# The steady part of a fused attention and FFN kernel: a written order, states times W_in four chunks at a time, softmax rows turned by 32x32 blocks and DMA

## The chip, the cores and the metric

The kernel runs on one core of a Trainium2 chip. The metric is the device time of one execution in microseconds. A core has a matrix engine (TensorE, PE in the profile, with its weight loads as PEld), a vector engine (VectorE, DVE), a scalar engine (ScalarE, ACT), and SyncE (SP), which here only issues DMA transfers; ScalarE can issue transfers too. Each engine works through its own list of instructions in order and waits on semaphores that other engines and transfers raise. TensorE writes to PSUM, which has eight banks of 128 x 512 fp32; everything else lies in SBUF.

## The reference

There are 8 batches. In each, 8 heads hold 512 tokens and 32 states of 64 numbers. Tokens read the states, states read the tokens, and all rows then go through one FFN with W_in (512 x 2048), a bounded square and W_out (2048 x 512):

```python
scores = scale * x @ state.T             # (512, 32) per head
a = softmax(scores);  xread = a @ state
a2 = softmax(scores.T); sread = a2 @ x   # (32, 512) @ (512, 64)
rows = concatenate([xread, sread])       # 544 rows per batch, 512 wide
h = rows @ w_in
g = where(h >= 1, h, where(h <= -1, 0, (h + 1) ** 2 / 4))
out = g @ w_out
```

The result has 4352 rows of 512 in fp32. The kernel keeps this precision by splitting operands into a high part (fp32r) and the rest, and by adding three products: high x high, high x low, low x high.

## The kernel before

**The work of a batch.** The states are multiplied by W_in first, so that `a @ (state @ w_in)` takes the place of `(a @ state) @ w_in`. W_in has 8 chunks of 256 columns. `sw_product` (L416) makes states x W_in for `n` chunks: 16 small matmuls (64 x 32) per chunk into the PSUM tile `sw`, which has the tag "mm" (one buffer of two banks). `sw_high` (L436, ScalarE) and `sw_low` (L440, VectorE) split it into two SBUF tiles, of which there are two pairs. In the steady part a pair of chunks is made at a time, `sw_make(nb, nj, 2)`.

**The FFN.** A step (b, j) treats 256 of the 2048 hidden columns of batch b, so a batch has 8 steps. `g1` (L509) makes two products of 6 matmuls into two PSUM banks (tag "h", two buffers), then on ScalarE relu of each and one square of both, on VectorE `bound` of each (it reads the h bank a last time), then `high` (ScalarE) and `low` (VectorE). `g2` (L520) multiplies the result of the step before by W_out: 24 matmuls into four PSUM banks (tag "acc", four buffers). After the last step of a batch, `store` (L547) copies each acc bank to SBUF on ScalarE and sends it out through ScalarE's DMA queue.

**The attention of the next batch** runs beside the FFN in pieces, the generator `Attention.steps` (L379): scores into mm (16 matmuls, `sc`); VectorE's 32x32 block transposes, the softmax over states, and the transpose back give the tokens' side (`ath`, `atl`); maximum and exponential straight from the scores give the states' side `e2`. `turn2` (L327) turns `e2` in 8 TensorE transposes (128 x 128) into the mm banks (`e2p`), `keep_turned` copies it back to SBUF on ScalarE, `read2` (L342) multiplies it by the tokens in 64 small matmuls (`sr`), `scale2` (VectorE) divides by the sums, `keep2` (L365) is one TensorE transpose (`rt`), and `keep` copies it into `srT`. For batches 2 to 7 `sr` and `rt` lie in h banks. The states' rows of all 8 batches go through the FFN at the end as "batch 8" (four steps; there W_in itself is split by `wi_split`, L449).

**What sets the order.** The start (batch 0 and the attention of batch 1) is laid out by a planner, `Plan`, and issued in its order inside `tc.manual_schedule()`. The steady part (L794 to L827) is issued after that block has been closed: the loop gives the instructions, and the framework's scheduler places them on each engine. A step is g1, then g2 of the step before, then `between_steps`: an sw pair after every even step, and one piece of attention after steps 1, 3, 4 and 6. SP's queue carries the loads of the next batch (`load_xt`, `load_xn`, issued at step 0).

Of the kernel before, what the change touches and what calls it, by code (L numbers as in the profile page):

```python
# [137 lines left out]
def state_exchange_moe(  # L138
# [27 lines left out]
    NJ = NF // 2  # L166
# [45 lines left out]
    att_of = {}  # L212
# [12 lines left out]
    class Attention:  # L225
# [109 lines left out]
        def keep_turned(self):  # L335
# [3 lines left out]
            nc.vector.tensor_scalar_add(self.r2, self.sum2, 1e-9)  # L339
            nc.vector.reciprocal(out=self.r2, in_=self.r2)  # L340

        def read2(self):  # L342
            b = self.b
            xn = loaded.pop(("xn", b))
            if b < 2:
                sr = self.sr = ps_mm(f"sr{b}")
            else:
                sr = self.sr = ps_h(f"sr{b}").rearrange("p (q f) -> p q f", q=2)
            for q in range(2):
                for t in range(NT):  # L350
                    for pr in range(NPR):
                        c0 = t * P + pr * NS
                        nc.tensor.matmul(  # L353
                            sr[pr * NS:(pr + 1) * NS, q, :D], lhsT=self.e2[:, q, c0:c0 + NS],
                            rhs=xn[:, t, 2 * pr + q], start=t == 0, stop=t == NT - 1,
                        )
# [6 lines left out]
            )  # L363

        def keep2(self):  # L365
            if self.b < 2:
                self.rt = ps_mm(f"rt{self.b}")
            else:
                self.rt = ps_h(f"rt{self.b}").rearrange("p (q f) -> p q f", q=1)
            nc.tensor.transpose(  # L370
                out=self.rt[:, 0, :P], in_=self.rs.rearrange("p a d -> p (a d)"), identity=ident
            )
# [6 lines left out]
        def steps(self):  # L379
            self.scores()  # L380
            for q in range(2):
                self.turn(q)
            for q in range(2):
                self.top2(q)
            for q in range(2):
                self.exp2(q)
            yield
            for f in (self.top1, self.less1, self.exp1, self.sum1, self.inv1, self.norm1):
                for q in range(2):
                    f(q)  # L390
            self.turn2()
            self.keep_turned()
            yield
            for q in range(2):
                self.back(q)
                self.high1(q)
                self.rest(q)
            self.read2()
            self.scale2()
            yield  # L400
            self.keep2()
            self.keep()
            yield

# [6 lines left out]

    sw_of = {}

    def sw_product(b, c, n):  # L416

        pt = ps_mm(f"sw{b}_{c}")
        for i in range(n):
            for pr in range(NPR):  # L420
                for hh in range(2):
                    rows = slice(hh * 64, hh * 64 + 64)
                    nc.tensor.matmul(  # L423
                        pt[pr * NS:(pr + 1) * NS, hh, i * CI:(i + 1) * CI],
                        lhsT=sb[rows, b, pr], rhs=w32[c + i][rows, pr], start=True, stop=True,
                    )
# [4 lines left out]
        sw_of[b, c] = pt[:, :, :w], wh, wl  # L431
        for i in range(n):
            cols = slice(i * CI, (i + 1) * CI)
            chunk[b, c + i] = wh[:, :, cols], wl[:, :, cols]

    def sw_high(b, c):  # L436
        pt, wh, _ = sw_of[b, c]
        nc.scalar.copy(out=wh, in_=pt)

    def sw_low(b, c):  # L440
        pt, wh, wl = sw_of[b, c]
        nc.vector.tensor_tensor(out=wl, in0=pt, in1=wh.bitcast(F32), op=ALU.subtract)

    def sw_make(b, c, n):
        sw_product(b, c, n)
        sw_high(b, c)
        sw_low(b, c)
# [11 lines left out]
    class Hidden:  # L459
# [26 lines left out]
        def relu(self, i):  # L486
            nc.scalar.activation(out=self.u[:, i], in_=self.hs[i], func=AF.Relu, scale=0.5, bias=half)  # L487

        def square(self):
            nc.scalar.activation(out=self.u, in_=self.u, func=AF.Square)  # L490

        def bound(self, i):
            nc.vector.scalar_tensor_tensor(  # L493
# [15 lines left out]
    def g1(b, j):  # L509
        hid = Hidden(b, j)  # L510
        for i in range(2):
            hid.product(i)
            hid.relu(i)
        hid.square()
        for i in range(2):
            hid.bound(i)
        hid.high()
        hid.low()

    def g2(b, j, half=None):  # L520
# [12 lines left out]
        for i, t in pairs:  # L533
            f = 2 * per * j + i
            oh, ol = wo[f // 2][:, 0, f % 2], wo[f // 2][:, 1, f % 2]
            c0 = (i % per) * n + t * P
            lh, ll = (v[:, i // per, c0:c0 + P] for v in (gh, gl))
            a = acc[b][t]
            nc.tensor.matmul(a, lhsT=lh, rhs=oh, start=f == 0, stop=False)  # L539
            nc.tensor.matmul(a, lhsT=lh, rhs=ol, start=False, stop=False)  # L540
            nc.tensor.matmul(a, lhsT=ll, rhs=oh, start=False, stop=f == NF - 1)  # L541
            if last and i == 2 * per - 1:
                store(b, t)
# [3 lines left out]
    def store(b, t):  # L547
        if t == 0:
            outs[b] = rawp.tile([P, NT, DM], F32, tag="raw", name=f"o{b}")
        o = outs[b][:, t]  # L550
        if b == B and t % 2:
            nc.vector.tensor_copy(o, acc[b][t])
        else:
            nc.scalar.copy(out=o, in_=acc[b][t])  # L554
        if b < B:
            r0 = b * TOK + t * P
            nc.scalar.dma_start(out=out[r0:r0 + P, :], in_=o)
        else:
# [85 lines left out]
    atts = {}  # L644
# [140 lines left out]
        if j:  # L785
            g2_ops(0, j - 1, 1)
    sw_ops(1, 0, 2)
    import os
    with guard:
        plan.emit(warm, ("sc", 0, 0), ("g2", 0, 0, 0))  # L790

    steps = [(b, j) for b in range(1, B + 1) for j in range(NJ if b < B else NJ // 2)]  # L794

    def between_steps(b, j):

        if b < B:
            nb, nj = (b, j + 2) if j + 2 < NJ else (b + 1, 0)
            if j % 2 == 0 and nb < B:  # L800
                sw_make(nb, nj, 2)
            if j in (1, 3, 4, 6):
                next(att, None)

    def splits(b, j):
        if b == B:
            for c in (2 * j, 2 * j + 1):
                wi_split(c)

    for i, (b, j) in enumerate(steps):  # L810
        if j == 0:
            if b + 1 < B:
                loaded["xt", b + 1] = load_xt(b + 1)
                loaded["xn", b + 1] = load_xn(b + 1)
                att = Attention(b + 1).steps()
            elif b == B:
                sh, sl = (work.tile([P, NPR, B * NS], F32R, tag=t, name=f"s{t}") for t in ("ath", "atl"))
                src = srT.rearrange("p a b n -> p a (b n)")
                nc.vector.tensor_copy(sh, src)
                nc.vector.tensor_tensor(out=sl, in0=src, in1=sh.bitcast(F32), op=ALU.subtract)  # L820
                att_of[B] = (sh, sl)
        g1(b, j)
        if i + 1 < len(steps):
            splits(*steps[i + 1])
        g2(*(steps[i - 1] if i else (0, NJ - 1)))
        between_steps(b, j)
    g2(*steps[-1])  # L827


_INS = ["x", "xt", "state", "moe_w_in", "moe_w_out"]  # L830
# [40 lines left out]
```

## Time and profile before

| what | us |
|---|---|
| median of three runs | 666.8 (666.66 to 666.98) |
| profiled execution: span from first to last instruction | 664.4 |
| TensorE busy in it | 653.2 |
| VectorE / ScalarE busy in it | 339.9 / 362.8 |
| one period of the steady part (eight steps) | 73.88 |
| start, until the first step of batch 1 | some 98 |

The profiled execution's own time was not recorded apart from its span; the span is 2.4 us under the median, for what lies before the first and after the last instruction. The page gives each engine's busy time; a matmul's listed duration overlaps the next one's, so costs on TensorE are read as distances between starts. In a row of a timeline the first number is the start, the second the duration, both in us; in a row of groups the pair after the bar is total busy us and mean ns. In a row of stretches each engine has its busy time and its instructions, and the last three numbers are TensorE's granted clock, the share of DMA and GB/s.

### The profile page before, as it was taken

Reading aid. Unit: us, or ns where it says so; the run is one execution under the profiler, and the core shown is the slowest. Engines: PE = TensorE matmul, PEld = TensorE weight load, DVE = VectorE, ACT = ScalarE, POOL = GpSimd, SP = SyncE. Lnnn points to the kernel's source line nnn. Section 1 sums busy time; section 2 is a strip of 40 time slices with the busy share of each in tenths; the row PEclk is TensorE's granted clock in tenths of the full one; section 3 lists DMA queues with packets and bytes.
Section 4 is the critical chain, followed back from the end, with each engine's and each line's share of the span. In section 5 each row is a group of like instructions: output and inputs, shape, how many; then the busy total and the mean of one; then the engine's idle time right before and its main releaser. Section 6 shows DMA issues by size and latency. Waiting matters only on the chain.

```text
span 664.4 us, 10294 instructions
## 1 busy us (share of the span) xinstructions
PE 653.2 (98%) x4444; PEld 515.3 (78%) x4444; DVE 339.9 (51%) x489; ACT 362.8 (55%) x462; POOL 0.8 (0%) x7
## 2 busy tenths in 40 slices
PE   6999999999999999999999999999999999999997
PEld 6777777777778777777777877777778787778895
DVE  4999953933365334833375335733384343333431
ACT  4899845644556445644555444644555455454632
POOL 0000000000000000000000000000000000000000
PEclk9899999999999999999999999999999999999999
DMA  8896101110110102110110103010100001000101
GB/s 346 350 393 273 64 1 64 63 65 0 65 64 1 64 1 78 50 65 1 64 64 1 64 1 120 7 64 1 65 1 1 1 26 39 1 1 1 63 1 32
DMA packets 11085, 43.64 MB, mean 66 GB/s; under 512 B 1312, under 2 KB 1440, under 8 KB 7968
## 3 DMA queue, kind: packets, MB, share of 16 engines
q1 hardware_dynamic: 5952, 33.75, 13.3%
q10 hardware_dynamic: 5088, 9.24, 3.7%
q8 instruction: 34, 0.56, 0.3%
q14 instruction: 11, 0.09, 0.0%
HBM read 34.08 MB, written 8.91 MB: 65 GB/s over the span
## 4 chain that ended last, share of the span: by engine, by line
PE 92%; ACT 4%; DVE 2%; DMA 1%; issue 0%; ACTq 0%; SPq 0%
PE acc L539 18%; PE acc L541 18%; PE acc L540 18%; PE h L481 11%; PE h L482 9%; PE h L483 9%; PE sw L423 5%; DMA xt<-in_xt_dram 1%; PE sr L353 1%; PE sc L253 1%; PE e2p L333 1%; PE warmed L198 1%; ACT u L487 1%; ACT raw_i L593 1%; ACT gh L502 0%; ACT raw_o L593 0%
## 5 line engine op out<-in xcount | busy, mean ns | idle before, releaser
L539 PE MATMUL acc<-wo,gh 128*128 128x512 f32 x544 | 213.3, 392 | 0.0
L541 PE MATMUL acc<-wo,gl 128*128 128x512 f32 x544 | 211.8, 389 | 0.0
L540 PE MATMUL acc<-wo,gh 128*128 128x512 f32 x544 | 211.7, 389 | 0.0
L493 DVE SCALAR_TENSOR_TENSOR u<-u,h 128x512 f32<-128x512 f32 x136 | 87.4, 683 | 170.5 <-ACT u L490 170.2
L487 ACT ACTIVATE u<-h,half 128x512 f32<-128x512 f32 x136 | 93.7, 690 | 146.5 <-PE h L483 145.8
L539 PEld LDWEIGHTS acc<-wo,gh 128*128 128x128 f32 x544 | 102.2, 188 | 24.6 <-issue 3.7
L541 PEld LDWEIGHTS acc<-wo,gl 128*128 128x128 f32 x544 | 102.1, 188 | 21.6
L540 PEld LDWEIGHTS acc<-wo,gh 128*128 128x128 f32 x544 | 102.2, 188 | 20.8
L507 DVE TENSOR_TENSOR gl<-u,gh 128x1024 fp32r<-128x1024 f32 x68 | 83.2, 1223 | 60.8 <-ACT gh L502 60.8
L502 ACT CAST gh<-u 128x1024 fp32r<-128x1024 f32 x68 | 71.5, 1052 | 67.0 <-DVE u L493 67.0
L490 ACT ACTIVATE u<-u 128x1024 f32<-128x1024 f32 x68 | 72.3, 1064 | 1.6
L423 PE MATMUL sw<-w,sb 64*32 64x256 f32 x1024 | 35.9, 383 | 2.2 <-DVE w L601 2.2
L423 PEld LDWEIGHTS sw<-w,sb 64*32 64x32 f32 x1024 | 15.1, 106 | 18.2 <-issue 11.3
L554 ACT COPY o<-acc 128x512 f32<-128x512 f32 x33 | 18.9, 583 | 12.0 <-PE acc L541 12.0
L481 PE MATMUL h<-ath,sw_4h 128*128 128x512 f32 x60 | 25.3, 422 | 0.1
L481 PE MATMUL h<-ath,sw_2h 128*128 128x512 f32 x60 | 24.9, 415 | 0.0
L481 PE MATMUL h<-ath,sw_0h 128*128 128x512 f32 x60 | 24.4, 410 | 0.0
L481 PE MATMUL h<-ath,sw_6h 128*128 128x512 f32 x60 | 23.9, 398 | 0.0
L483 PE MATMUL h<-atl,sw_4h 128*128 128x512 f32 x60 | 23.5, 392 | 0.0
L482 PE MATMUL h<-ath,sw_4l 128*128 128x512 f32 x60 | 23.5, 391 | 0.0
L483 PE MATMUL h<-atl,sw_6h 128*128 128x512 f32 x60 | 23.5, 391 | 0.0
L482 PE MATMUL h<-ath,sw_0l 128*128 128x512 f32 x60 | 23.5, 391 | 0.0
(173 smaller groups left out, 733.3 us busy)
## 6 DMA issues: line engine op xcount, KB each, us to landing
raw_i<-in_moe_w_in_dram SPq DMA_DIRECT2D x8, 1024.0 KB, 6.5
raw_o<-in_moe_w_out_dram SPq DMA_DIRECT2D x8, 1024.0 KB, 8.6
xn<-in_x_dram SPq DMA_DIRECT2D x8, 1024.0 KB, 4.7
out_dram<-o ACTq DMA_DIRECT2D x32, 256.0 KB, 2.0
xt<-in_xt_dram SPq DMA_DIRECT2D x15, 512.0 KB, 4.5
xt<-in_xt_dram ACTq DMA_DIRECT2D x1, 512.0 KB, 7.8
sb<-in_state_dram SPq DMA_DIRECT2D x1, 448.0 KB, 12.0
out_dram<-o SPq DMA_DIRECT2D x4, 64.0 KB, 1.7
```

What stands on the lines that cost most here:

```text
L423: nc.tensor.matmul(pt[pr * NS:(pr + 1) * NS, hh, i * CI:(i + 1) * CI], lhsT=sb[rows, b, pr], rhs=w32[c + i][rows, pr], start=True, stop=True,)
L481: nc.tensor.matmul(o, lhsT=wh[:, k, sl], rhs=ah[:, k], start=first, stop=False)
L482: nc.tensor.matmul(o, lhsT=wl[:, k, sl], rhs=ah[:, k], start=False, stop=False)
L483: nc.tensor.matmul(o, lhsT=wh[:, k, sl], rhs=al[:, k], start=False, stop=last)
L487: nc.scalar.activation(out=self.u[:, i], in_=self.hs[i], func=AF.Relu, scale=0.5, bias=half)
L490: nc.scalar.activation(out=self.u, in_=self.u, func=AF.Square)
L493: nc.vector.scalar_tensor_tensor(out=self.u[:, i], in0=self.u[:, i], scalar=1.0, in1=self.hs[i], op0=ALU.min, op1=ALU.max,)
L502: nc.scalar.copy(out=gh, in_=self.u)
L507: nc.vector.tensor_tensor(out=gl, in0=self.u, in1=gh.bitcast(F32), op=ALU.subtract)
L539: nc.tensor.matmul(a, lhsT=lh, rhs=oh, start=f == 0, stop=False)
L540: nc.tensor.matmul(a, lhsT=lh, rhs=ol, start=False, stop=False)
L541: nc.tensor.matmul(a, lhsT=ll, rhs=oh, start=False, stop=f == NF - 1)
```

## The change

It does six things.

1. The whole steady part is issued inside the manual block, so each engine works in the order in which the loop is written. Pieces of attention and other small work are put into lists (`later`) and issued at three places of a step: "half" (inside g1 between its two products), "mid" (after g1), "end" (after g2).
2. `sw_make` takes two pairs at once, after steps 3 and 7, between the two halves of that step's g2: the first pair in the two h banks (`apart`), the second in mm. The casts and subtractions of the first pair are done bank by bank.
3. For batches 2 to 7 `turn2` and `keep_turned` give way to `turn_blocks` (two block transposes on VectorE) and `shuffle`: 16 transfers on SP's queue that put the 32-row blocks in their places. `turn2` stays in the planned start.
4. `sr` and `rt` lie in mm for all batches.
5. The square is done in halves, each right after its relu; the first bound follows before the second product is issued.
6. The stores of batches 0 to 7 go out on SP's queue, no longer on ScalarE's. The splits of W_in for "batch 8" move to the new places too.

```diff
+        def turn_blocks(self, q):
+            if q == 0:
+                self.blocks = work.tile([P, 2, S], F32, tag="tmp", name=f"eb{self.b}")
+            nc.vector.transpose(out=self.blocks[:, q], in_=self.e2[:, q])
+
+        def shuffle(self):
...
+            nc.vector.tensor_scalar_add(self.r2, self.sum2, 1e-9)
+            nc.vector.reciprocal(out=self.r2, in_=self.r2)
+            src, dst = (
+                v.rearrange("p q (t r n) -> p (q t) r n", r=NPR, n=NS) for v in (self.blocks, self.e2)
+            )
+            for r in range(NPR):
+                for pr in range(NPR):
+                    nc.sync.dma_start(
+                        out=dst[r * NS:(r + 1) * NS, :, pr], in_=src[pr * NS:(pr + 1) * NS, :, r]
+                    )
...
-            if b < 2:
-                sr = self.sr = ps_mm(f"sr{b}")
-            else:
-                sr = self.sr = ps_h(f"sr{b}").rearrange("p (q f) -> p q f", q=2)
+            sr = self.sr = ps_mm(f"sr{b}")
...
+    def sw_product(b, c, n, apart=False):
+
+        if apart:
+            banks = [ps_h(f"sw{b}_{c}_{hh}") for hh in range(2)]
+        else:
+            pt = ps_mm(f"sw{b}_{c}")
+            banks = [pt[:, hh] for hh in range(2)]
...
     def sw_high(b, c):
+        for pt, wh, _ in sw_of[b, c]:
+            nc.scalar.copy(out=wh, in_=pt)
...
+    def sw_make(b, cs):
+
+        for i, c in enumerate(cs):
+            sw_product(b, c, 2, apart=i == 0 and len(cs) == 2)
+        for c in cs:
+            sw_high(b, c)
+            sw_low(b, c)
...
-        def square(self):
-            nc.scalar.activation(out=self.u, in_=self.u, func=AF.Square)
+        def square(self, i=None):
+            u = self.u if i is None else self.u[:, i]
+            nc.scalar.activation(out=u, in_=u, func=AF.Square)
...
             hid.product(i)
             hid.relu(i)
-        hid.square()
-        for i in range(2):
+            hid.square(i)
             hid.bound(i)
+            if i == 0:
+                issue("half", b, j)
...
-            nc.scalar.dma_start(out=out[r0:r0 + P, :], in_=o)
+            nc.sync.dma_start(out=out[r0:r0 + P, :], in_=o)
...
+    def attention(b):
...
+        later("end", b - 1, 1, (att_start, b))
+        at("end", 1, "turn 0", "turn 1", "top2 0")
+        at("mid", 2, "exp2 0", "top2 1", "exp2 1", "top1 0", "top1 1", "turn_blocks 0")
+        at("mid", 3, "turn_blocks 1", "shuffle")
+        at("end", 3, "less1 0", "less1 1")
+        at("mid", 4, "exp1 0", "exp1 1", "sum1 0", "sum1 1", "inv1 0", "inv1 1")
+        at("end", 4, "norm1 0")
+        at("mid", 5, "norm1 1", "back 0", "back 1", "high1 0", "rest 0", "high1 1", "rest 1")
+        at("end", 5, "read2", "scale2")
+        at("end", 6, "keep2", "keep")
...
+    for b in range(2, B):
+        attention(b)
+    later("end", 1, 0, (sw_make, 1, (2,)))
+    later("mid", B - 1, 6, (states_split,))
+    later("mid", B - 1, NJ - 2, (wi_split, 0))
+    later("mid", B - 1, NJ - 1, (wi_split, 1))
+    for j in range(NJ // 2 - 1):
+        later("half", B, j, (wi_split, 2 * j + 2))
+        later("mid", B, j, (wi_split, 2 * j + 3))
+
     with guard:
         plan.emit(warm, ("sc", 0, 0), ("g2", 0, 0, 0))
...
+        for i, (b, j) in enumerate(steps):
+            if j == 0 and b + 1 < B:
                 loaded["xt", b + 1] = load_xt(b + 1)
                 loaded["xn", b + 1] = load_xn(b + 1)
...
+            prior = steps[i - 1] if i else (0, NJ - 1)
+            ahead = (b, 4) if j == 3 else (b + 1, 0)
+            if i == 0:
+                g2(*prior, 0)
+            g1(b, j)
+            issue("mid", b, j)
+            if i == 0:
+                g2(*prior, 1)
+            elif j % 4 == 3 and ahead[0] < B:
+                g2(*prior, 0)
+                sw_make(ahead[0], (ahead[1], ahead[1] + 2))
+                g2(*prior, 1)
+            else:
+                g2(*prior)
+            issue("end", b, j)
+        g2(*steps[-1])
```

More of the change, by code (lines that the diff above doesn't have):

```diff
@@ L340, in keep_turned @@
             nc.vector.reciprocal(out=self.r2, in_=self.r2)
+        def turn_blocks(self, q):
[3 more added lines that the diff above has]
+        def shuffle(self):
+            b = self.b
+            self.r2 = small.tile([P, 2], F32, tag="r2", name=f"r2_{b}")
+            nc.vector.tensor_scalar_add(self.r2, self.sum2, 1e-9)
[8 more added lines that the diff above has]
+                    )
         def read2(self):
@@ L365, in keep2 @@
         def keep2(self):
[L366 to L369, printed above, removed]
+            self.rt = ps_mm(f"rt{self.b}")
             nc.tensor.transpose(
@@ L377, in keep @@
             )
[L379 to L403, printed above, removed]
     def split_tiles(name):
@@ L414, in state_exchange_moe @@
     sw_of = {}
-    def sw_product(b, c, n):
-        pt = ps_mm(f"sw{b}_{c}")
+    def sw_product(b, c, n, apart=False):
[4 more added lines that the diff above has]
+            banks = [pt[:, hh] for hh in range(2)]
         for i in range(n):
@@ L423, in sw_product @@
                     nc.tensor.matmul(
-                        pt[pr * NS:(pr + 1) * NS, hh, i * CI:(i + 1) * CI],
+                        banks[hh][pr * NS:(pr + 1) * NS, i * CI:(i + 1) * CI],
                         lhsT=sb[rows, b, pr], rhs=w32[c + i][rows, pr], start=True, stop=True,
@@ L430, in sw_product @@
         )
-        sw_of[b, c] = pt[:, :, :w], wh, wl
+        if apart:
+            sw_of[b, c] = [(banks[q][:, :w], wh[:, q], wl[:, q]) for q in range(2)]
+        else:
+            sw_of[b, c] = [(pt[:, :, :w], wh, wl)]
         for i in range(n):
@@ L436, in sw_high @@
     def sw_high(b, c):
-        pt, wh, _ = sw_of[b, c]
-        nc.scalar.copy(out=wh, in_=pt)
+        for pt, wh, _ in sw_of[b, c]:
+            nc.scalar.copy(out=wh, in_=pt)
     def sw_low(b, c):
[L441 to L447, printed above, removed]
+        for pt, wh, wl in sw_of[b, c]:
+            nc.vector.tensor_tensor(out=wl, in0=pt, in1=wh.bitcast(F32), op=ALU.subtract)
+    def sw_make(b, cs):
[4 more added lines that the diff above has]
+            sw_low(b, c)
     def wi_split(c):
@@ L787, in state_exchange_moe, with later, issue, at @@
     sw_ops(1, 0, 2)
-    import os
+    steps = [(b, j) for b in range(1, B + 1) for j in range(NJ if b < B else NJ // 2)]
+    background = {}
+    def later(place, b, j, *items):
+        for f, *a in items:
+            background.setdefault((place, b, j), []).append((f, a))
+    def issue(place, b, j):
+        for f, a in background.get((place, b, j), ()):
+            f(*a)
+    def attention(b):
+        def at(place, j, *names):
+            for name in names:
+                f, *q = name.split()
+                later(place, b - 1, j, (lambda f=f, q=q: getattr(atts[b], f)(*map(int, q)),))
+        later("end", b - 1, 1, (att_start, b))
[8 more added lines that the diff above has]
+        at("end", 6, "keep2", "keep")
@@ new lines, in states_split @@
+    def states_split():
+        sh, sl = (work.tile([P, NPR, B * NS], F32R, tag=t, name=f"s{t}") for t in ("ath", "atl"))
+        src = srT.rearrange("p a b n -> p a (b n)")
+        nc.vector.tensor_copy(sh, src)
+        nc.vector.tensor_tensor(out=sl, in0=src, in1=sh.bitcast(F32), op=ALU.subtract)
+        att_of[B] = (sh, sl)
+    for b in range(2, B):
[3 more added lines that the diff above has]
+    later("mid", B - 1, NJ - 2, (wi_split, 0))
@@ L789, in state_exchange_moe @@
+    later("mid", B - 1, NJ - 1, (wi_split, 1))
+    for j in range(NJ // 2 - 1):
+        later("half", B, j, (wi_split, 2 * j + 2))
+        later("mid", B, j, (wi_split, 2 * j + 3))
     with guard:
         plan.emit(warm, ("sc", 0, 0), ("g2", 0, 0, 0))
[L794 to L812, printed above, removed]
+        for i, (b, j) in enumerate(steps):
+            if j == 0 and b + 1 < B:
                 loaded["xt", b + 1] = load_xt(b + 1)
                 loaded["xn", b + 1] = load_xn(b + 1)
[L815 to L826, printed above, removed]
@@ L827, in state_exchange_moe @@
-    g2(*steps[-1])
+            prior = steps[i - 1] if i else (0, NJ - 1)
[10 more added lines that the diff above has]
+                g2(*prior, 1)
+            else:
+                g2(*prior)
```

## The prediction

> **What bounds the kernel now.** I read the page first, then the busy time by stretches, then TensorE's timeline over one batch of the steady part.
>
> ```profile
> span 664.4 us, 10294 instructions
> PE 653.2 (98%) x4444; PEld 515.3 (78%) x4444; DVE 339.9 (51%) x489; ACT 362.8 (55%) x462; POOL 0.8 (0%) x7
> PE 92%; ACT 4%; DVE 2%; DMA 1%; issue 0%; ACTq 0%; SPq 0%
> ```
>
> TensorE is 98% busy and 92% of the chain that ended last; the other engines stand near half. The stretches say where the missing 2% lies:
>
> ```profile
> 54.00:115.00 61.00, 60.82 (x428) 46.27 (x434) 43.44 (x59) 43.25 (x55) 0.00 (x0) 1.00 0.25 95
> 115.00:484.00 369.00, 368.96 (x2525) 287.52 (x2522) 178.05 (x266) 192.95 (x250) 0.00 (x0) 1.00 0.12 44
> ```
>
> From 115 us on TensorE has no idle time worth naming (368.96 of 369.00) at a granted clock of 1.00. So a microsecond taken off TensorE's list there is a microsecond off the end, unless the new order makes TensorE wait; and a wait of TensorE is lost in full. One period, the eight steps of a batch, is
>
> ```profile
> 262.67:336.55 73.88, 73.87 (x513) 57.53 (x518) 35.66 (x54) 38.59 (x50) 0.00 (x0) 1.00 0.12 44
> ```
>
> 73.88 us. Its parts are read as distances between starts, because a matmul's own duration (0.39) overlaps the next:
>
> ```profile
> 262.24 0.39 PE L541 MATMUL acc<-wo,gl 128*128 128x512 f32 x1
> 262.55 1.09 PE L253 MATMUL sc<-xt,sb 64*32 64x512 f32 x16
> 263.91 0.39 PE L482 MATMUL h<-ath,sw_2l 128*128 128x512 f32 x1
> ...
> 266.44 0.39 PE L539 MATMUL acc<-wo,gh 128*128 128x512 f32 x1
> ...
> 271.65 0.39 PE L541 MATMUL acc<-wo,gl 128*128 128x512 f32 x1
> 271.97 1.09 PE L423 MATMUL sw<-w,sb 64*32 64x256 f32 x32
> 273.00 0.50 PE L481 MATMUL h<-ath,sw_2h 128*128 128x512 f32 x1
> 273.33 0.40 PE L482 MATMUL h<-ath,sw_2l 128*128 128x512 f32 x1
> ...
> 281.06 0.39 PE L541 MATMUL acc<-wo,gl 128*128 128x512 f32 x1
> 281.29 1.03 PE L333 MATMUL e2p<-ident,e 128*128 128x128 f32 x8
> 282.40 0.40 PE L482 MATMUL h<-ath,sw_4l 128*128 128x512 f32 x1
> ...
> 290.12 0.39 PE L541 MATMUL acc<-wo,gl 128*128 128x512 f32 x1
> 290.43 1.09 PE L423 MATMUL sw<-w,sb 64*32 64x256 f32 x32
> 291.46 1.10 PE L353 MATMUL sr<-xn,e 128*32 128x64 f32 x64
> 292.49 0.50 PE L481 MATMUL h<-ath,sw_4h 128*128 128x512 f32 x1
> ...
> 294.16 0.50 PE L481 MATMUL h<-ath,sw_4h 128*128 128x512 f32 x1
> ...
> 295.65 0.40 PE L539 MATMUL acc<-wo,gh 128*128 128x512 f32 x1
> ...
> 309.04 0.39 PE L541 MATMUL acc<-wo,gl 128*128 128x512 f32 x1
> 309.36 1.09 PE L423 MATMUL sw<-w,sb 64*32 64x256 f32 x32
> 310.38 0.33 PE L370 MATMUL rt<-ident,rs 128*128 128x128 f32 x1
> 310.78 0.39 PE L482 MATMUL h<-ath,sw_6l 128*128 128x512 f32 x1
> ```
>
> An FFN matmul takes (271.65 − 266.44)/23 = 0.2265; g1 (12) is 2.72, g2 (24) 5.44. What an insertion costs is the distance from the last matmul before it to the second one after it, less two plain steps (0.453): **sc** 1.67 − 0.45 = 1.22; **one sw pair** 1.68 − 0.45 = 1.23 (1.03 of its own, 0.20 for going in and out); **e2p** 1.34 − 0.45 = 0.89; **sw with rt** 1.74 − 0.45 = 1.29; **sw with sr**, from 290.12 to 295.65, is 5.53 for 13 plain steps (2.94), so 2.59. In that last one 0.3 is a wait: the second half of g1 starts at 294.16, because sr sits in an h bank until VectorE's scale (L361) has read it. Per period this makes 1.22 + 2 × 1.23 + 0.89 + 1.29 + 2.59 = 8.45 beside 8 × 8.16 = 65.3 of FFN.
>
> **The change part by part.** Batches 2 to 7 take their attention in the six periods of steps b = 1 to 6. After the last of them two plain sw pairs follow (for b = 7). Now: 6 × 8.45 + 2 × 1.23 = 53.2.
>
> *Removed.* The six e2p groups go. Not all TensorE transposes do: turn2 stays in the plan for batches 0 and 1, and the single transpose rt stays for every batch.
>
> *Four chunks at a time.* The same 26 pairs come as 13 batches of 64 matmuls. How 64 in one go run is not in the trace. The nearest rows are a group of 16 and one of 32:
>
> ```profile
> 61.16 0.59 PE sw L423 x16
> ```
>
> 32 take 1.03, 16 take 0.59, so 16 more of the same shape cost 0.44, and a batch is 1.23 + 0.88 = 2.11. The other end: sr directly behind sw costs its full 1.03 (291.46 to 292.49), so 2.26. I take 2.11, since the second pair has the shape of the first and only another bank.
>
> *sr and rt moved to the mm banks, each alone.* The 0.3 wait goes, but both lose their neighbour: sr 1.03 + 0.20 = 1.23. rt beside a pair costs 1.29 − 1.23 = 0.06; alone at most its 0.33 and 0.1 around it, so 0.06 to 0.43; I take 0.25, since the entry and exit no longer lie with a pair. sr's first matmul now waits for up to sixteen transfers instead of one copy; checking semaphores that have long risen I put at 0 to 0.3 each time (as large as rt's whole record), taken as 0.05.
>
> After: 6 × (1.22 + 1.28 + 0.25) + 13 × 2.11 = 16.5 + 27.4 = 43.9, so **9.3 us less**. With each unknown at its worse end it is 6 × (1.22 + 1.53 + 0.43) + 13 × 2.26 = 48.5, 4.7 less; at its better end 6 × (1.22 + 1.23 + 0.06) + 27.4 = 42.5, 10.7 less.
>
> *Waits that the written order adds.* Each engine takes its list in order, so I followed one step with the rows of before; T is the start of g2 (295.65):
>
> ```profile
> 295.85 0.69 ACT L487 ACTIVATE u<-h,half 128x512 f32<-128x512 f32 x1 [0.97 <-PE h L483]
> 296.57 1.06 ACT L490 ACTIVATE u<-u 128x1024 f32<-128x1024 f32 x1
> 299.04 1.05 ACT L502 CAST gh<-u 128x1024 fp32r<-128x1024 f32 x1 [1.41 <-DVE u L493]
> ...
> 297.66 1.28 DVE L493 SCALAR_TENSOR_TENSOR u<-u,h 128x512 f32<-128x512 f32 x2 [3.56 <-ACT u L490]
> 300.12 1.23 DVE L507 TENSOR_TENSOR gl<-u,gh 128x1024 fp32r<-128x1024 f32 x1 [1.17 <-ACT gh L502]
> ...
> L280 ACT ACTIVATE z<-z 128x512 f32<-128x512 f32 x16 | 9.3, 631 | 0.9 <-DVE z L275 0.9
> L300 DVE STREAM_TRANSPOSE zt<-z 128x512 f32<-128x512 f32 x16 | 11.3, 704 | 0.0
> L438 ACT CAST sw_0h<-sw 128x512 fp32r<-128x512 f32 x1 | 0.6, 578 | 0.0
> L442 DVE TENSOR_TENSOR sw_0l<-sw,sw_0h 128x512 fp32r<-128x512 f32 x1 | 0.7, 684 | 0.0
> ```
>
> The first pair of a batch goes to the two h banks, after half of g2, at T + 2.8. They come free when the second bound has read them. Before, that is 298.94, T + 3.3, half a microsecond too late. With the square in halves (0.63 by the L280 row instead of 1.06) and the first half done during the second product, it runs relu T + 0.2, square 0.9 to 1.6, bound to about T + 2.3: in time by 0.5. The split costs ScalarE 2 × 0.63 − 1.06 = 0.2 per step, beside a ScalarE at 55%.
>
> Late next are the h banks for the following g1, due at T + 2.8 + 2.1 + 2.7 = T + 7.6. High and low of this step end near T + 4.7; turn_blocks 1 (0.70) and the two small operations of shuffle bring VectorE to T + 5.7; the casts of the two banks (0.58 each, from T + 4.0) are done by 5.2; the two subtractions (0.68 each) end at T + 7.0. Cover 0.6 us. In step 2 top2 1, two top1 and turn_blocks 0 keep VectorE until T + 7.3; its next step starts 8.2 after T. mm is free: exp2 1 ends a step before the batch, scale2 a step before rt.
>
> *Shuffle and stores on SP's queue.* Sixteen transfers of 32 KB, from SBUF to SBUF in runs of 128 B, behind them nothing due soon (the loads of the next batch and the four stores have a step or more). No row shows such a transfer; the nearest are an issue pair and the 64 KB stores:
>
> ```profile
> 116.07 1.06 SPq L217 DMA_DIRECT2D xt<-in_xt_dram  x2
> out_dram<-o SPq DMA_DIRECT2D x4, 64.0 KB, 1.7
> ```
>
> 0.53 per issue and 1.7 to landing: 16 × 0.53 + 1.7 = 10.2 us from T + 5.4 of step 3. read2 comes at the end of step 5, that is 5.44 + 2.11 + 2 × 8.16 = 23.9 after T. It has 18.5, so it is covered by 8; sr would wait above 1.16 us per transfer. Stores leave ScalarE's queue for SP's: nothing on the path.
>
> The Trainium skill, page "DMA: Bandwidth & Descriptors", section "Rules for kernel authors", says to join many small transfers into one large, since under 64 KB one pays mostly overhead. The 64 KB row with its 1.7 us agrees; by that rule alone the shuffle would be the mistake of this change, and its time would be that of the first rival below. The same page ("Why small descriptors are slow (HBM only)") exempts SBUF-to-SBUF transfers from the penalty on short runs, which no run here shows.
>
> *The sum.* 664.4 − 9.3 = 655.1 of span. The median stands 2.4 above the span (666.8 against 664.4), so 657.5.
>
> **Rivals.** *The shuffle is late (slower).* If the sixteen transfers, which fill interleaved columns of one tile, go one after the other, each with issue and landing, they take 16 × 1.7 = 27 to 16 × 2.23 = 36 us where 18.5 are free: sr, and with it all of TensorE, waits 9 to 17 us in each of six periods, 51 to 103. The middle gives 657.5 + 77 = 735. It decides from 1.16 us per transfer; the gain is eaten at 1.26 (9.3/6/16 more). For it: the small length of the runs, and sixteen destinations in one tile. Against it: low and high of a weight chunk (L580, L593) also write alternate words of one tile, and the list of waits has no row in which one waits for the other.
>
> *The h banks are late.* If the split square buys nothing, because ScalarE or VectorE holds older work at that moment, the bound ends at T + 3.3 and each batch waits 0.5: 13 × 0.5 = 6.5 us, 664.0. For it: only 0.5 of cover. Against it: the list of steps above, in which both engines are free at T.
>
> *The order costs what the removal brings.* Waits of 1.2 us in each of the eight steps of a period, or fewer and longer ones, would leave 666.8. Against it: gl is due 8.2 after T and ready at 4.7.
>
> **How the numbers follow.** Forecast 0.74, h banks late 0.12, shuffle late 0.08, gain eaten 0.04, and 0.02 for a time below the better end. The predicted time is the forecast's, 657.5. The better end is 666.8 − 10.7 = 656.1, the worse end 662.1; up to 664.0 the range also holds most of the h-bank case, which makes 0.84. Under 0.2% (1.3 us) a measurement of this kernel tells nothing from no change. Faster is forecast, h banks and the low end, 0.88; same 0.04; slower 0.08.
>
> **What would show it.** Right: TensorE still without idle time after 115 us at clock 1.00, no L333 after the plan, 13 groups of 64 L423 with 2.1 us each, a period of 72.3 us, no wait of sr on a DMA. Wrong: rows of PE or PEld waiting for DMA at L353 (first rival), for DVE L49x at L423 or for L442's line at the first product (second), or sw groups of 2.3 and more.

## The result, and the profile after

The changed kernel takes 655.4 us (655.2 to 655.7, four runs) beside 666.7 for the kernel before on the same chip: a ratio of 0.983, with an interval of 0.9815 to 0.9843. Faster, as forecast, and by 11.3 instead of 9.3 us. (The 666.7 is somewhat high: on the two later occasions on which both kernels were measured, the kernel before took 666.4 and 666.2, and the gain was 10.5 and 10.9.)

The page of the changed kernel, its span, its busy times, the chain that ended last by engine, and a row of its DMA issues:

```profile
span 653.6 us, 10398 instructions
PE 644.3 (99%) x4396; PEld 514.7 (79%) x4396; DVE 354.7 (54%) x514; ACT 371.5 (57%) x529; POOL 0.8 (0%) x7
PE 92%; ACT 4%; DVE 2%; DMA 1%; issue 0%; ACTq 0%; SPq 0%
...
e<-eb SPq DMA_DIRECT2D x96, 32.0 KB, 1.9
```

TensorE has 48 matmuls and some 9 us less, and still makes 92% of the chain: no other engine has become the bound. The 96 transfers of the shuffle (16 for each of six batches) land 1.9 us after their issue in the median.

The busy time of one period, from the scores of one batch to those of the next, in the changed kernel:

```profile
114.54:186.77 72.23, 72.23 (x499) 57.28 (x498) 37.94 (x57) 39.52 (x59) 0.00 (x0) 1.00 0.17 52
```

It was 73.88 before. TensorE is busy in all of it, at a granted clock of 1.00. A wait can still hide inside the duration of a group (e4 below has such a one), so the insertions are checked by distances too, further down.

Where the 10.8 us between the two spans went follows from where the scores of batches 2 and 7 and the first product with `wj` (the start of "batch 8") begin. TensorE's timeline of the changed kernel, then of the kernel before:

```profile
114.54 1.09 PE L253 MATMUL sc<-xt,sb 64*32 64x512 f32 x16
...
475.74 1.09 PE L253 MATMUL sc<-xt,sb 64*32 64x512 f32 x16
...
599.02 0.28 PE L478 MATMUL h<-sath,wj0h 128*128 128x256 f32 x1
```

```profile
114.88 1.09 PE L253 MATMUL sc<-xt,sb 64*32 64x512 f32 x16
...
484.13 1.09 PE L253 MATMUL sc<-xt,sb 64*32 64x512 f32 x16
...
609.30 0.28 PE L481 MATMUL h<-sath,wj0h 128*128 128x256 f32 x1
```

Five periods take 361.20 instead of 369.25, 8.05 less. The stretch from there to `wj`, which holds the sixth period and the last products of states and W_in, takes 123.28 instead of 125.17, 1.89 less. Together **9.9 us is the list of the steady part**. Another 0.3 lies ahead of it (114.54 against 114.88). The rest is the end. VectorE's last copy in the changed kernel and in the one before:

```profile
649.54 0.69 DVE L551 COPY o<-acc 128x512 f32<-128x512 f32 x1 [6.50 <-DMA out_dram<-o]
```

```profile
659.85 0.69 DVE L552 COPY o<-acc 128x512 f32<-128x512 f32 x1 [5.44 <-DMA out_dram<-o]
```

From that copy to the end of the span are 653.6 − 649.54 = 4.06 and 664.4 − 659.85 = 4.55: 0.5 less. It does not lie in the stores: by the landing records of the two traces, the last store lands 3.08 us after the start of that copy in both kernels. After the landing come 0.93 us in the changed kernel and 1.46 in the one before, in which the engines close the program. The closing instructions of SyncE, of the changed kernel and then of the one before (shortest, median and longest in ns, first and last start in us):

```profile
L899 SPq DRAIN  x3: 7/7/7, 652.8 to 653.1; - x3
```

```profile
L867 SPq DRAIN  x3: 7/7/120, 663.5 to 664.0; - x3
```

In the kernel before, SyncE's first DRAIN takes 120 ns instead of 7 and starts 0.43 us after SyncE's last closing wait has ended, instead of 0.04. These two make the half microsecond.

The new insertions, as TensorE's timeline of the changed kernel shows them (start, duration):

```profile
126.59 0.39 PE L538 MATMUL acc<-wo,gh 128*128 128x512 f32 x1
...
129.08 0.39 PE L540 MATMUL acc<-wo,gl 128*128 128x512 f32 x1
129.40 1.96 PE L414 MATMUL sw<-w,sb 64*32 64x256 f32 x64
131.29 0.50 PE L538 MATMUL acc<-wo,gh 128*128 128x512 f32 x1
131.63 0.40 PE L539 MATMUL acc<-wo,gh 128*128 128x512 f32 x1
...
150.28 0.39 PE L540 MATMUL acc<-wo,gl 128*128 128x512 f32 x1
150.60 1.10 PE L369 MATMUL sr<-xn,e 128*32 128x64 f32 x64
...
151.96 0.40 PE L479 MATMUL h<-ath,sw_6l 128*128 128x512 f32 x1
...
159.69 0.39 PE L540 MATMUL acc<-wo,gl 128*128 128x512 f32 x1
159.92 0.27 PE L383 MATMUL rt<-ident,rs 128*128 128x128 f32 x1
...
160.26 0.40 PE L479 MATMUL h<-ath,sw_6l 128*128 128x512 f32 x1
```

By the prediction's method (from the last matmul before to the second one after, less 0.45) a batch of 64 costs 2.10, sr 1.23 and rt 0.12. No row carries an idle time, and sr costs just what the prediction has for it without a wait (1.03 of its own and 0.20), so it did not wait.

### The profile page after: what moved, and what is told of

It is laid out like the page before. It is cut to its first block, busy times and chain, and to the rows that moved or that the text cites. A ratio compares the mean times of both kernels' runs of the same rounds, so it can differ in the third digit from the quotient of the medians.

```text
span 653.6 us, 10398 instructions
## 1 busy us (share of the span) xinstructions
PE 644.3 (99%) x4396; PEld 514.7 (79%) x4396; DVE 354.7 (54%) x514; ACT 371.5 (57%) x529; POOL 0.8 (0%) x7
## 4 chain that ended last, share of the span: by engine, by line
PE 92%; ACT 4%; DVE 2%; DMA 1%; issue 0%; ACTq 0%; SPq 0%
PE acc L538 19%; PE acc L539 18%; PE acc L540 18%; PE h L478 10%; PE h L480 10%; PE h L479 10%; PE sw L414 4%; DMA xt<-in_xt_dram 1%; PE sr L369 1%; PE sc L253 1%; PE warmed L198 1%; ACT u L484 1%; ACT raw_i L592 1%; ACT gh L500 0%; ACT raw_o L592 0%; ACT u L488 0%
## 5 line engine op out<-in xcount | busy, mean ns | idle before, releaser
L491 DVE SCALAR_TENSOR_TENSOR u<-u,h 128x512 f32<-128x512 f32 x136 | 92.8, 687 | 191.5 <-ACT u L488 191.5
L488 ACT ACTIVATE u<-u 128x512 f32<-128x512 f32 (+1 forms) x128 | 84.5, 660 | 3.8
L414 PE MATMUL sw<-w,sb 64*32 64x256 f32 x1024 | 33.1, 381 | 2.2 <-DVE w L600 2.2
L414 PEld LDWEIGHTS sw<-w,sb 64*32 64x32 f32 x1024 | 17.7, 106 | 14.3 <-issue 6.7
L553 ACT COPY o<-acc 128x512 f32<-128x512 f32 x33 | 18.0, 587 | 10.9 <-PE acc L540 10.9
L480 PE MATMUL h<-atl,sw_2h 128*128 128x512 f32 x60 | 23.4, 391 | 0.0
L479 PE MATMUL h<-ath,sw_6l 128*128 128x512 f32 x60 | 23.4, 390 | 0.0
L480 PE MATMUL h<-atl,sw_0h 128*128 128x512 f32 x60 | 23.4, 389 | 0.0
```

What stands on the lines that cost most here:

```text
L414: nc.tensor.matmul(banks[hh][pr * NS:(pr + 1) * NS, i * CI:(i + 1) * CI], lhsT=sb[rows, b, pr], rhs=w32[c + i][rows, pr], start=True, stop ...
L479: nc.tensor.matmul(o, lhsT=wl[:, k, sl], rhs=ah[:, k], start=False, stop=False)
L480: nc.tensor.matmul(o, lhsT=wh[:, k, sl], rhs=al[:, k], start=False, stop=last)
L488: nc.scalar.activation(out=u, in_=u, func=AF.Square)
L491: nc.vector.scalar_tensor_tensor(out=self.u[:, i], in0=self.u[:, i], scalar=1.0, in1=self.hs[i], op0=ALU.min, op1=ALU.max,)
```

## Experiments

Each run is measured beside the kernel before on the same chip; that one's median was 666.4, 666.0 and 666.2 on the three occasions.

**TensorE's transposes back (e1).** The changed kernel with `turn2` and `keep_turned` in step 4, and no shuffle:

```diff
-        at("mid", 2, "exp2 0", "top2 1", "exp2 1", "top1 0", "top1 1", "turn_blocks 0")
-        at("mid", 3, "turn_blocks 1", "shuffle")
+        at("mid", 2, "exp2 0", "top2 1", "exp2 1", "top1 0", "top1 1")
...
-        at("end", 4, "norm1 0")
+        at("end", 4, "norm1 0", "turn2", "keep_turned")
```

> The changed kernel, but for batches 2 to 7 the eight TensorE transposes and ScalarE's copy are back (end of step 4) in place of the block transposes and the sixteen transfers. My theory: TensorE never waits after 115 us, so its list sets the end, and a group e2p costs 0.89 going in and out: 6 x 0.89 = 5.3 us more than 655.4, so 660.7. Rival: in the new order the transposes would lie beside other work and the gain comes from elsewhere: 655.4.

Measured: 661.4 us, ratio 0.9922 (0.9907 to 0.9937). The period, by the busy time in stretches of this kernel:

```profile
114.11:187.26 73.15, 73.15 (x506) 58.11 (x505) 36.92 (x55) 40.54 (x60) 0.00 (x0) 1.00 0.12 44
```

The period grows by 0.92, the price that the prediction had read from the kernel before (0.89); six of them are the 5.5 us between this run and the changed kernel.

**The batch cut in two (e2).** One pair between the halves of g2, the other after it:

```diff
             elif j % 4 == 3 and ahead[0] < B:
                 g2(*prior, 0)
-                sw_make(ahead[0], (ahead[1], ahead[1] + 2))
+                sw_make(ahead[0], (ahead[1],), True)
                 g2(*prior, 1)
+                sw_make(ahead[0], (ahead[1] + 2,))
```

> The changed kernel, but each batch of four chunks is cut in two: the first pair stays between the halves of g2, the second goes behind the second half. My theory: going in and out of the small matmuls costs 0.22 per insertion, and a second pair directly behind the first saves a drain of 0.16 too (64 take 1.89, 32 take 1.03): 13 x (2 x 1.24 - 2.15) = 4.3 us more, 659.7. Rival: the small matmuls cost what they cost wherever they lie: 655.4.

Measured: 660.0 us, 0.9901 (0.9886 to 0.9916). The period of this kernel:

```profile
114.61:187.52 72.91, 72.91 (x499) 56.74 (x499) 37.95 (x57) 39.72 (x59) 0.00 (x0) 1.00 0.17 51
```

The period grows by 0.68 for two extra insertions, 0.34 each; two pairs apart cost 2 × 1.23 = 2.46, a batch 2.10. The joining is worth what the distances say.

**The square whole again (e4).** One square after both relus, both bounds after it:

```diff
             hid.relu(i)
-            hid.square(i)
-            hid.bound(i)
             if i == 0:
                 issue("half", b, j)
+        hid.square()
+        for i in range(2):
+            hid.bound(i)
         hid.high()
```

> The changed kernel, but relu of both halves, then one square of both, then both bounds, as before. My theory: the second bound ends at T + 3.3 (T is the start of g2), the first pair of a batch wants its h banks at T + 2.8, so TensorE waits 0.5 in each of 13 batches: 6.5 us more, 661.9. ScalarE's 0.2 us per step saved are worth nothing. Rival: the banks come free early enough anyway, or the halves themselves cost ScalarE more than they bring: 655.4 or less.

Measured: 662.6 us, 0.9941 (0.9926 to 0.9956). The period, then a batch on TensorE, then the two bounds ahead of it on VectorE, all of this kernel:

```profile
114.82:188.05 73.23, 73.23 (x498) 57.55 (x497) 37.03 (x58) 37.73 (x51) 0.00 (x0) 1.00 0.17 51
```

```profile
129.68 2.50 PE L414 MATMUL sw<-w,sb 64*32 64x256 f32 x64
132.11 0.50 PE L539 MATMUL acc<-wo,gh 128*128 128x512 f32 x1
```

```profile
128.88 1.28 DVE L491 SCALAR_TENSOR_TENSOR u<-u,h 128x512 f32<-128x512 f32 x2 [1.88 <-ACT u L488]
```

The bounds end at 130.16, half a microsecond after the group has begun, and the group takes 2.43 to the next matmul instead of 1.89. The wait hides inside the group's own duration: TensorE still shows as busy all through. The weight loads show it. A row of this kernel's list of waits (total us, times, longest):

```profile
PEld sw L414 <- DVE u L491: 9.9, 26, 0.4
```

Twice in each of the 13 batches the weight loads wait for a bound; the changed kernel's list has no such row. This is the sign that the prediction named for its second rival. The rival's 0.5 per batch, twice per period, comes exactly when the split is taken away.

**The changed kernel again (a0).**

> The changed kernel itself on the same chip as the others: 655.4, so that its variants are compared with it in one place. What lies outside the span is 1.8 to 2.4 us if that differs from run to run by chance, as I believe; if it is a property of the kernel it is 1.8 again, with 2.4 for the kernel before.

Measured: 655.9 us (655.5 to 656.9), 0.9845 (0.9829 to 0.9862). The profiled execution took 655.5 with a span of 653.7, so 1.8 lie outside the span. It is no property of the changed kernel: of the 39 later executions of the kernel before whose time and span are both on record (b0's among them), 36 have 1.8 to 2.1 us outside the span (three have 2.8 to 3.2). The 2.4 of the section on the time before was the median of three executions less the span of another.

**The steady loop given to the framework's scheduler (e5).** The same calls in the same loop, issued after the manual block has been closed:

```diff
     with guard:
         plan.emit(warm, ("sc", 0, 0), ("g2", 0, 0, 0))
-        for i, (b, j) in enumerate(steps):
...
-        g2(*steps[-1])
+    for i, (b, j) in enumerate(steps):
...
+    g2(*steps[-1])
```

> The changed kernel with the same steps, but the steady loop stands outside the manual block, so the framework's scheduler places it on each engine, as before. My theory: the time comes from what TensorE has on its list and from the place of the batches; as long as the scheduler leaves TensorE's list nearly as written and the h banks are free in time, it is within 2 us of 655.9. Rival: the written order is what keeps TensorE from waiting; without it the batches find the h banks busy, and 13 waits of half a microsecond and more bring 662 or above.

Measured: 655.6 us, 0.984 (0.9825 to 0.9854). The period of this kernel:

```profile
114.59:186.81 72.22, 72.22 (x498) 57.28 (x497) 37.23 (x57) 39.25 (x59) 0.00 (x0) 1.00 0.17 52
```

Equal to the changed kernel's 72.23. With the calls in this sequence (the lists for "half", "mid" and "end" are in both), it makes no difference to the time whether the engines follow them word for word or the scheduler places them (it lets the shuffle of the first period start at 124.39 instead of 131.89); the rival that the manual block brought the time falls.

**sr and rt back in the h banks (e3).**

```diff
-            sr = self.sr = ps_mm(f"sr{b}")
+            if b < 2:
+                sr = self.sr = ps_mm(f"sr{b}")
+            else:
+                sr = self.sr = ps_h(f"sr{b}").rearrange("p (q f) -> p q f", q=2)
...
-            self.rt = ps_mm(f"rt{self.b}")
+            if self.b < 2:
+                self.rt = ps_mm(f"rt{self.b}")
+            else:
+                self.rt = ps_h(f"rt{self.b}").rearrange("p (q f) -> p q f", q=1)
```

> The changed kernel, but sr and rt of batches 2 to 7 lie in the h banks again. My theory: the next g1 waits for the bank that VectorE's scale still reads, as before (0.3 us of wait, and a scale that now stands behind the five operations at the middle of step 5): 6 x 0.3 = 1.8 us or somewhat more, 657.7 to 659. Rival: which banks sr takes does not matter, the wait of before came from its place beside a pair: 655.9.

Measured: 656.3 us, 0.985 (0.9836 to 0.9865); the period is 72.40. TensorE's timeline of this kernel, the matmuls around the place where g1 needs the bank that sr holds, then VectorE's scale of sr in this kernel and in the kernel before:

```profile
153.06 0.50 PE L484 MATMUL h<-ath,sw_6h 128*128 128x512 f32 x1
153.40 0.39 PE L485 MATMUL h<-ath,sw_6l 128*128 128x512 f32 x1
```

```profile
152.73 0.28 DVE L380 TENSOR_TENSOR rs<-sr,r 128x128 f32<-128x128 f32 x1
```

```profile
293.82 0.28 DVE L361 TENSOR_TENSOR rs<-sr,r 128x128 f32<-128x128 f32 x1
```

The matmul at 153.06 takes 0.50 and the next starts 0.34 later instead of 0.23: the wait is there, but only some 0.16 in all (the period has 0.17 more), half of the 0.3 in the kernel before. VectorE has older work in both; here the scale starts 1.18 us after the first matmul behind sr (151.55), there 1.33 (292.49), so the bank comes free 0.15 earlier. More was expected; the move to mm is worth 0.16 × 6 = 1 us, less than the 1.3 us under which a time of this kernel tells nothing, so the row and the period show it, not the time.

**The shuffle later in the written order (e6).** Its call stands after the sums and inverses of step 4 instead of in step 3:

```diff
-        at("mid", 3, "turn_blocks 1", "shuffle")
+        at("mid", 3, "turn_blocks 1")
...
-        at("mid", 4, "exp1 0", "exp1 1", "sum1 0", "sum1 1", "inv1 0", "inv1 1")
+        at("mid", 4, "exp1 0", "exp1 1", "sum1 0", "sum1 1", "inv1 0", "inv1 1", "shuffle")
```

> The changed kernel, but the sixteen transfers are issued in the middle of step 4 instead of step 3. In the trace of the changed kernel they take 11.6 us of SP's queue and 1.9 to land, and the last lands 5.8 us before sr. My theory: they begin 9.6 us later (after VectorE's divisions of step 4), so sr waits some 4 us in each of six periods, all of it lost: 655.9 + 24 = 680, with 14 to 30 by the bounds. Rival: TensorE has other work that fills a late sr: 655.9.

Measured: 656.2 us, 0.9852 (0.9834 to 0.987). The expectation failed. SP's queue of this kernel, then two rows of VectorE:

```profile
133.47 11.82 SPq L357 DMA_DIRECT2D e<-eb  x16
```

```profile
132.70 0.70 DVE L345 STREAM_TRANSPOSE eb<-e 128x512 f32<-128x512 f32 x1
...
144.89 0.10 DVE L350 TENSOR_SCALAR r<-sum 128x2 f32<-128x2 f32 x1
```

The call's VectorE part did move (144.89), the transfers did not: they start at 133.47, as soon as the second block transpose has ended (133.40). SP had nothing else in its list ahead of them, so a later place in the written order delays nothing. This run did not make the shuffle late, and so says nothing of its cover.

**The shuffle alone, in the kernel before (e7).** Nothing else of the change:

```diff
-            self.turn2()
-            self.keep_turned()
+            self.turn_blocks(0)
+            self.turn_blocks(1)
+            self.shuffle()
```

> The kernel before with one part of the change alone: for batches 2 to 7 block transposes and the sixteen transfers in place of the TensorE transposes, in the same pieces of the old order (both after step 3, sr after step 4). My theory: 6 x 0.89 = 5.3 us less where the transfers land in time; but there they begin after VectorE has done the softmax of a whole piece, and sr comes one step later, some 8 us, where the transfers need 13.5: sr waits 4 to 6 us in each period, so 6 x (5 - 0.89) = 25 us slower, 691 (678 to 700). Rival: the part stands on its own feet and brings 5.3: 661.2.

Measured: 660.1 us, 0.991 (0.9893 to 0.9926), the rival's number. SP's queue and sr on TensorE in this kernel:

```profile
126.27 10.52 SPq L357 DMA_DIRECT2D e<-eb  x16
```

```profile
142.66 1.10 PE L372 MATMUL sr<-xn,e 128*32 128x64 f32 x64
```

The expected wait did not come, because the transfers depend only on the exponentials, which are done long before the place of `turn2`: they begin at 126.27, end near 126.27 + 10.52 + 1.9 = 138.7, and sr comes at 142.66. The kernel before gets 5.9 us shorter by this; half a microsecond of that is the end of the program, which is short here too (see a1 and b0). So the exchange of e2p for the shuffle is worth 5.4 us, and needs none of the rest.

**The shuffle really late (e6b).** So the second block transpose, which feeds the transfers, is moved too:

```diff
-        at("mid", 3, "turn_blocks 1", "shuffle")
...
-        at("mid", 4, "exp1 0", "exp1 1", "sum1 0", "sum1 1", "inv1 0", "inv1 1")
+        at("mid", 4, "exp1 0", "exp1 1", "sum1 0", "sum1 1", "inv1 0", "inv1 1", "turn_blocks 1", "shuffle")
```

> The changed kernel, but the second block transpose, which every transfer waits for, comes on VectorE after the divisions of step 4, so that the transfers begin some 12 us later (in the run before this only their place in the written order was moved, and since SP had nothing else to do they began as early as ever). My theory: they begin near 144 on the scale of the changed kernel's first period, need 13.5 us, and land 6.9 us after sr is due (150.6): 6 x 6.9 = 41 us more, 697 (685 to 705), all of it as idle time of TensorE ahead of sr. Rival: the wait is filled by other work: 656.

Measured: 700.3 us, 1.0509 (1.0494 to 1.0525). SP's queue of this kernel, the row of its list of waits (total us, times, longest), TensorE's timeline, and the stretch from sr's first matmuls to some way behind it (the number after the five engines is the granted clock):

```profile
145.42 10.52 SPq L357 DMA_DIRECT2D e<-eb  x16
```

```profile
PE sr L369 <- DMA e<-eb: 26.5, 23, 4.6
```

```profile
155.55 0.27 PE L369 MATMUL sr<-xn,e 128*32 128x64 f32 x2 [3.49 <-DMA e<-eb]
...
157.38 1.88 PE L369 MATMUL sr<-xn,e 128*32 128x64 f32 x58 [0.26 <-DMA e<-eb]
...
159.79 0.63 PE L479 MATMUL h<-ath,sw_6l 128*128 128x512 f32 x1
160.22 0.63 PE L480 MATMUL h<-atl,sw_6h 128*128 128x512 f32 x1
...
162.77 0.40 PE L480 MATMUL h<-atl,sw_6h 128*128 128x512 f32 x1
```

```profile
155.95:162.70 6.75, 6.10 (x70) 4.84 (x71) 0.29 (x1) 0.48 (x1) 0.00 (x0) 0.50 0.87 280
```

Now sr waits, and what the first rival feared is seen: the whole of TensorE stands still for the transfers. The last of them lands near 145.42 + 10.52 + 1.9 = 157.8, so a start 13.5 us later than in the changed kernel (131.89) eats the cover and more. The time is in the expected range, but not all of it is idle time: 26.5 us of waits are 4.4 per period where 6.9 were expected, and the period grew by 7.2 (79.44 in the mean of five). That the sum came out near is luck. A lower granted clock, read below, makes a good part of the other 2.8; how much in the mean of the periods was not worked out.

**A step further: fewer insertions (e8).** sr is put directly in front of the batch of step 7, rt in front of the batch of step 3, and `low` of step 7 after sr's scale:

```diff
-        at("end", 5, "read2", "scale2")
-        at("end", 6, "keep2", "keep")
...
-            g1(b, j)
+            joined = j == NJ - 1 and b + 1 < B
+            hid_ = g1(b, j, low=not joined)
...
                 g2(*prior, 0)
+                if joined:
+                    atts[b + 1].read2()
+                    atts[b + 1].scale2()
+                    hid_.low()
+                elif b > 1:
+                    atts[b].keep2()
+                    atts[b].keep()
                 sw_make(ahead[0], (ahead[1], ahead[1] + 2))
```

> The changed kernel, but sr goes directly in front of the batch after step 7 and rt in front of the batch after step 3, so that five insertions per period become three; VectorE's scale of sr is put ahead of low in that step, so that mm is free for the second pair. My theory: an insertion costs TensorE 0.22 for going in and out whatever it holds: sr 1.25 falls to 1.03 and rt 0.13 to 0.05, 6 x 0.30 = 1.8 us less, 653.9 beside 655.7. Rival: sr in front of the pair holds mm until the scale is done, and the second pair waits as much as is won: 655.7 or above.

Measured: 653.7 us (653.4 to 654.5), 0.9809 (0.9795 to 0.9822), 1.6 us under the changed kernel of the same occasion. Its period, and TensorE where sr and the batch now touch:

```profile
114.77:186.61 71.84, 71.84 (x497) 57.31 (x497) 37.93 (x57) 39.23 (x58) 0.00 (x0) 1.00 0.18 52
```

```profile
164.11 0.39 PE L542 MATMUL acc<-wo,gl 128*128 128x512 f32 x1
164.42 1.10 PE L369 MATMUL sr<-xn,e 128*32 128x64 f32 x64
165.46 1.96 PE L414 MATMUL sw<-w,sb 64*32 64x256 f32 x64
...
167.68 0.39 PE L541 MATMUL acc<-wo,gh 128*128 128x512 f32 x1
```

Together they cost 167.68 − 164.11 − 0.45 = 3.12, apart 1.23 + 2.10 = 3.33: one going in and out (0.2) saved. The period falls by 0.3 to 0.4. This version beats both kernels: each of its five runs is below each of the four of the changed kernel.

**Both kernels once more (a1, b0).**

> The changed kernel again, beside the next two and in as many rounds: 655.4 to 655.9, with periods of 72.24 us and 4.4 us from the last matmul's start to the end of the span, as in its two profiles so far.

> The kernel before, to see whether its first profile is typical: there the last matmul's start stands 4.97 us ahead of the end of the span, in every later profile of any variant 4.44. My theory: that half microsecond is chance in the last transfers, so 4.4 here, a span near 664.0 and periods of 73.85. Rival: it belongs to the kernel before: 4.97 again.

Measured: 655.3 us, 0.9831 (0.9818 to 0.9844), for the changed kernel; 666.2, 0.9998 (0.9989 to 1.0007), for the kernel before. The span of the kernel before is 664.5 in this run. Its VectorE's last copy:

```profile
659.93 0.69 DVE L552 COPY o<-acc 128x512 f32<-128x512 f32 x1 [5.44 <-DMA out_dram<-o]
```

From the copy to the end are 4.6 us again, and 653.7 − 649.69 = 4.0 in a1. I had held the difference for chance, and that was wrong; the rival that it belongs to the kernel stands. From the start of the last matmul to the end of the span the kernel before has 664.5 − 659.51 = 5.0 here. e7, the kernel before with only the shuffle, has 658.4 − 653.91 = 4.5, so it needs neither the queue of the stores nor the written order; e1, without the shuffle, has 658.7 − 654.21 = 4.5, so it doesn't need the shuffle either. All twelve profiles of other kernels, the changed one among them, have the short end. The closing steps of SyncE, shown above, are where it lies; why SyncE pauses there in the kernel before stays open.

## Why the prediction was right or wrong

**The bound and the kind of result: right.** TensorE's list of the steady part sets the time, and a microsecond off it is a microsecond off the end. e1, e2 and e4 put back one part each and lose what the distances gave.

**The costs.** A batch of 64: taken 2.11, measured 2.10. sr alone: 1.23, and 1.23. e2p: 0.89, and 0.92 when put back. Checking the semaphores of the transfers: 0.05, measured as nothing. **rt alone was mis-sized**: 0.25 was taken between 0.06 and 0.43, and it is 0.12. Why it pays less for going in and out than the groups of small tiles was not tried. With the semaphore checks this is 0.18 per period, 1.1 us in six periods; what the distances leave unaccounted takes 0.5 of it back. The list gave 9.9 where 9.3 was forecast, inside the 4.7 to 10.7 of its bounds.

**The waits.** The split square brings the second bound to its end 2.3 us after T, as worked out. The changed kernel's VectorE, with T = 126.59 (the first row of g2 above):

```profile
128.18 0.69 DVE L491 SCALAR_TENSOR_TENSOR u<-u,h 128x512 f32<-128x512 f32 x1 [0.61 <-ACT u L488]
...
131.99 1.27 DVE L436 TENSOR_TENSOR sw_4l<-sw,sw_4h 128x512 fp32r<-128x512 f32 x2
```

The bound ends at 128.87, T + 2.28, half a microsecond ahead of the group at 129.40. The subtractions end at 133.26, T + 6.7 (7.0 in the prediction), and the next g1 is due at T + 7.6. e4 shows that this cover is needed: without the split the rival's 0.5 per batch appears.

**The shuffle.** It was covered, but by less than the prediction said. SP's queue of the changed kernel:

```profile
131.89 11.63 SPq L357 DMA_DIRECT2D e<-eb  x16
```

The start is right (T + 5.3 against 5.4). Sixteen issues take 0.73 us each in the mean, not the 0.53 read from a plain load, and land 1.9 later: 145.4, where sr stands at 150.60. That leaves 5.2 us, not 8. The first rival (each transfer waiting for the one before) did not occur: its least step was 1.7 us.

**What failed** is the last line of the sum: "664.4 − 9.3 = 655.1 of span", then 2.4 on top. It held everything outside the steady part at nothing and took the 2.4 for a fixed time outside the span. The runs show something else in three places. The end became 0.5 shorter (4.97 us from the last matmul's start to the end in both profiles of the kernel before, 4.4 to 4.5 in all others). What lies outside the span is 1.8 in the changed kernel (655.4 − 653.6) and 1.8 to 2.1 in nearly all executions of the kernel before; the 2.4 compared different executions and was half a microsecond too much. The head was 0.3 shorter, which can't be told from chance: where batch 2's scores begin varies between the profiles from 114.1 to 115.0 (116.1 in e6 and 115.9 in e6b). With the list alone at its 9.9 the sum would have been 664.4 − 9.9 + 2.4 = 656.9, above the better end of 656.1; these three terms, not the list, carry the time below it, where the prediction had put a chance of 0.02. Each should have had a bound of some half a microsecond. What makes the end shorter stays open; where it lies is shown above.

**The reasons behind the change.** e5 shows that the manual block brings nothing by itself here. The gain is the exchange of e2p (5.5 us by e1, 5.4 by e7), the joining of pairs (4.1 by e2, and only with the split square, e4), and 1 us or less for the banks of sr and rt (e3). They add up to about the 9.9 of the list; the end's 0.5 comes on top. The stores on SP's queue were not tried alone.

## What to carry to other kernels

Where one engine is busy throughout, cost an edit by distances between starts, insertion by insertion, and count how often its stream of equal matmuls is interrupted: each interruption by small-tile matmuls cost 0.2 us here, and joining them was worth 4.1 us beside 5.5 for the transposes that went. Moving a call in the written order is not moving the work: in e6 the idle queue started the transfers when their data were there, so ask what feeds them. And give the parts that "don't change" (head, end, the time outside the span) a bound of their own in the sum, and take a span and a time from the same execution.

## What the runs showed of the hardware

**A wait costs more than its length.** In the first period of e6b TensorE stood idle for 3.49 us unbroken, and then worked for two matmuls at a time between waits of 0.26. The granted clock in the stretch from 155.95 to 162.70 is 0.50. The last 58 matmuls of sr take 1.88 us there, where all 64 take 1.10 in the changed kernel. The matmuls behind them start 0.43 us apart (159.79 to 160.22) instead of 0.227: eight starts in a row are so, from 159.79 to 162.77 in seven spacings, and 1.4 us are lost by that alone. The Trainium skill, page "TensorE: Matmul & The Clock Gate", section "Part 1: The HAM clock gate (the "warmup" mystery)", says that an idle stretch of about 3.4 us lowers the clock to half, until TensorE has been busy for about as long. The trace agrees in the half (0.43 / 0.227 = 1.9), but not in the lengths: in the second period the granted clock falls from 1.00 to 0.50 at 234.43, 2.3 us into a wait of 3.84, and the half clock lasts 6.8 us in four of the six periods and 3.4 in two. A wait of some 4 us on the path therefore has to be priced with this on top.

**Small transfers from SBUF to SBUF** of 32 KB take 0.66 us (e7, 10.52 for 16) to 0.74 us (e6, 11.82) of SP's queue each in the mean of sixteen, against 0.53 for the loads that the prediction had. In the changed kernel the issue itself takes 0.61 us in the median and up to 1.69.

**A transfer's place in the program and its start are apart**: in e6 by 11 us. And the 0.5 us at the end of the program lies behind the last store's landing (0.93 us to the end of the span, 1.46 in the kernel before); its cause remains open.
